# Two homes for two of three tiles of a block's rounded input, and conversions whose scaling names no activation table

## The chip, the cores and the metric

The kernel runs on one core of a Trainium2 chip. The metric is the device time of one execution in microseconds (us), as the median of several runs; lower is better. PE is TensorE, ACT is ScalarE, DVE is VectorE, POOL is GpSimd, SP is SyncE, which issues all DMA transfers.

## The reference, cut to what matters

A decaying linear attention (4 batches, 8 heads, 768 tokens, head size 48) feeds two feed-forward layers of 384 to 2048 to 384 for each of 3072 tokens. All values are float32, and the weights arrive as float64.

```python
for t in range(S):
    state = alpha[:, :, t, :, None] * state + np.einsum('bhd,bhe->bhde', k[:, :, t], v[:, :, t])
    y[:, :, t] = np.einsum('bhd,bhde->bhe', q[:, :, t], state)
x = y.transpose(0, 2, 1, 3).reshape(B * S, H * D)
# layer 1
h = x @ w_in1
g = (a0 + a1*h + a2*h**2 + a3*h**3) / (1 + |b0|*|h| + |b1|*h**2 + 1e-6)
x = g @ w_out1
# layer 2
h = x @ w_in2
g = h * tanh(log1p(exp(h)))
out = g @ w_out2
```

## The kernel before

**Tiling.** The tokens are cut into 6 blocks of 4 x 128. A phase (l, c) is layer l of block c; the 12 phases run in the order of `PHASES`. A phase has 16 steps, one for each 128 columns of the hidden size. A step is a hidden product (`hidden_mms`, L652: three groups k = 0, 1, 2 of three matmuls of 512 columns into one of three PSUM banks), the nonlinear function on ACT, DVE and POOL (`hidden`, L667 to L689), the split of its result g (`split_g`), and an output product (`out_mms`, L701, nine matmuls, into banks 5 to 7). Every float32 factor is split into a rounded part and the rest ("high" and "low"), and three products stand for one.

**The rounded input.** `split_x` makes of a block's input three tiles `xh0`, `xh1`, `xh2` by a rounding copy (L220 on ACT, L222 on DVE) and three tiles `xl0` to `xl2` by a subtraction on DVE (L646). Each of the six tiles has one home, so a phase's copy `xh0` waits until the last hidden product of the phase before has read `xh0`; the same goes for the others.

**Weights.** `load_w` turns a pair of weight tiles from float64 to the split form, 32 times. Sixteen of them (layer 1) fall into the opening and phase (0, 0), sixteen (layer 2) into phases (0, 1) and (1, 0). Each begins on ACT with L327, a scaling written as the function Abs with the table "ln"; after it come either two ACT instructions (L340, L341) and one of DVE (L343), or three of DVE (L329, L331, L333), as `E_CV` says. Later phases stream the converted tiles from DRAM (L371, L372).

**Tables.** ACT's function in layer 2 is Mish (L689), in layer 1 Ln and Exp. `hidden` and L327 name their table, and each change of the named table puts an `ACT_TABLE_LOAD` into ACT's queue (L689 and L799).

**Attention.** Twelve units `attn_unit` (block c, two batches each) work through six levels (L461 on PE, L476 and L496 on DVE, L491 and L485 on ACT), an outer product (L540), outputs (L575 or L611). The first block's two units run before the first hidden product; the others lie among the phases. Filler matmuls (L745) occupy PE until the first hidden product.

**Ends of phases.** `evacuate` copies the three output banks into the ring of three buffers `u` and writes them to DRAM (L714, L712, L715). The first steps of the next layer-1 phase write the same ring (L667).

**What sets the order.** `Plan` gets each instruction with a due time and lists them engine by engine in a small schedule of its own; the due times come from the numbers at the top (`T_PH`, `AT_P`, `D_X`, `LAG`, `W_LEAD` and so on), the engine of a choice from the strings (`E_CV`, `E_HC`, `E_GL0`, `E_GL1`). Each engine then runs its list strictly in order, and SP issues transfers strictly in order.

## Time and profile before

| | |
|---|---|
| median of 3 runs | 1007.2 us (1005.48 to 1007.83) |
| profiled execution, its own time | 1007.53 us |
| its span, first to last instruction | 1005.7 us |
| mean granted TensorE clock | 0.995 |
| PE busy | 965.0 us (96%) |
| DVE busy | 657.2 us (65%) |
| ACT busy | 622.4 us (62%) |
| POOL busy | 309.5 us (31%) |

The time of an execution is its span and some 1.8 us around it. PE's busy time counts pipelined matmuls, so 96% is not 96% of what PE could do: back to back, nine matmuls of 512 columns start 2.04 us after the nine before them. What a change can win here is time in which PE waits.

### The profile page before, as it was taken

To read this page: it belongs to the slowest core of one execution; us is meant where nothing else is said; L and a number is where in the kernel's file an instruction comes from. 1 tells how busy PE (TensorE), PEld (TensorE's weight loads), DVE (VectorE), ACT (ScalarE), POOL (GpSimd) and SP (SyncE) were. 2 spreads that over 40 slices of the span, in tenths; PEclk is the share of its full clock that TensorE was granted. 3 is DMA by queue.
4 is the path that set the end of the run, shared out by engine and by line. 5 is a ranking of instruction groups with operands and counts; after the bars stand their busy time and mean duration, and the time that the engine had idled before them with its cause. 6 is when DMAs were issued, how large, how long until landed. Compare 5 with 4: busy or idle time off the path is not lost.

```text
span 1005.7 us, 24495 instructions
## 1 busy us (share of the span) xinstructions
PE 965.0 (96%) x10370; PEld 779.1 (77%) x10370; DVE 657.2 (65%) x850; ACT 622.4 (62%) x1048; POOL 309.5 (31%) x234
## 2 busy tenths in 40 slices
PE   7998999899999999999999999999999999999998
PEld 6776877677787878888878787767788878888886
DVE  6778999799998899724589733799951189400000
ACT  2787978798878798521498623386621299633332
POOL 2034666442500234334334300143322300043332
PEclk9999999999999999999999999999999999999999
DMA  8385747665768868558638655847446555465530
GB/s 323 120 288 211 261 134 273 220 189 207 254 237 308 299 214 280 166 191 257 211 107 277 192 185 155 292 118 256 118 135 207 149 155 147 136 220 147 176 110 31
DMA packets 75756, 199.98 MB, mean 199 GB/s; under 512 B 8192, under 2 KB 34944, under 8 KB 74112
## 3 DMA queue, kind: packets, MB, share of 16 engines
q1 hardware_dynamic: 75648, 198.43, 60.6%
q8 instruction: 81, 1.33, 0.5%
q14 instruction: 27, 0.22, 0.1%
HBM read 166.94 MB, written 31.46 MB: 197 GB/s over the span
## 4 chain that ended last, share of the span: by engine, by line
PE 64%; DVE 19%; ACT 9%; issue 5%; POOL 2%; DMA 1%; SPq 0%; ACTq 0%; DVEq 0%; POOLq 0%
PE bank L701 29%; PE bank L652 27%; PE pair L461 3%; DVE zp L685 3%; DVE gg L213 2%; DVE zp L676 2%; DVE zp L678 2%; PE bank L745 2%; DVE qka L476 1%; POOL zp L674 1%; PE pair L611 1%; ACT zp L680 1%; ACT zp L673 1%; ACT u L667 1%; ACT zp L684 1%
## 5 line engine op out<-in xcount | busy, mean ns | idle before, releaser
L701 PE MATMUL bank<-gg,wo 128*128 128x512 f32 x1728 | 430.5, 395 | 4.8 <-DVE gg L213 4.0
L701 PEld LDWEIGHTS bank<-gg,wo 128*128 128x128 f32 x1728 | 321.2, 188 | 75.6 <-DVE gg L213 7.7
L652 PE MATMUL bank<-xh,wih 128*128 128x512 f32 x576 | 230.2, 400 | 8.6 <-DVE zp L678 4.3
L652 PE MATMUL bank<-xl,wih 128*128 128x512 f32 x576 | 225.7, 392 | 3.0 <-DVE xl L646 3.0
L652 PE MATMUL bank<-xh,wl 128*128 128x512 f32 x576 | 225.5, 391 | 0.0
L215 POOL TENSOR_TENSOR gg<-zp,gg 128x512 fp32r<-128x512 f32 x80 | 111.8, 1398 | 268.8 <-ACT gg L220 162.7
L674 POOL TENSOR_TENSOR zp<-zp,u 128x512 f32<-128x512 f32 x80 | 125.4, 1568 | 193.1 <-ACT zp L673 192.9
L689 ACT ACTIVATE zp<-bank 128x512 f32<-128x512 f32 x96 | 57.1, 597 | 201.1 <-PE bank L652 201.0
L652 PEld LDWEIGHTS bank<-xh,wih 128*128 128x128 f32 x576 | 108.5, 188 | 34.3 <-DVE zp L678 6.5
L652 PEld LDWEIGHTS bank<-xl,wih 128*128 128x128 f32 x576 | 108.5, 188 | 25.6 <-DVE xl L646 4.4
L652 PEld LDWEIGHTS bank<-xh,wl 128*128 128x128 f32 x576 | 108.5, 188 | 23.3 <-DVE wl L213 0.4
L220 ACT CAST gg<-zp 128x512 fp32r<-128x512 f32 x144 | 89.3, 621 | 43.9 <-PE bank L701 31.0
L213 DVE TENSOR_TENSOR gg<-zp,gg 128x512 fp32r<-128x512 f32 x112 | 86.4, 776 | 34.3 <-ACT gg L220 33.8
L549 POOL TENSOR_TENSOR tmp<-X,qk 48x768 f32<-48x768 f32 x19 | 34.2, 1798 | 177.5 <-DVE X L554 98.2
L676 DVE SCALAR_TENSOR_TENSOR zp<-zp,sc,bank 128x512 f32<-128x512 f32 x96 | 70.9, 740 | 15.1 <-ACT zp L675 14.9
L685 DVE SCALAR_TENSOR_TENSOR zp<-zp,sc 128x512 f32<-128x512 f32 x80 | 72.9, 912 | 10.4 <-ACT zp L684 9.2
L461 PEld LDWEIGHTS pair<-qka 48*64 48x64 f32 (+4 forms) x3840 | 53.7, 125 | 32.1 <-issue 12.0
L680 ACT ACTIVATE zp<-zp,c 128x512 f32<-128x512 f32 x96 | 69.4, 725 | 12.0 <-POOL zp L674 11.9
L667 ACT ACTIVATE u<-bank 128x512 f32<-128x512 f32 x96 | 56.9, 594 | 29.8 <-PE bank L652 25.6
L222 DVE CAST gg<-zp 128x512 fp32r<-128x512 f32 x48 | 25.3, 527 | 75.4 <-ACT zp L689 67.8
L675 ACT ACTIVATE zp<-bank,sc 128x512 f32<-128x512 f32 x96 | 66.1, 688 | 13.1 <-PE bank L652 9.4
L678 DVE SCALAR_TENSOR_TENSOR zp<-zp,sc,bank 128x512 f32<-128x512 f32 x96 | 71.2, 743 | 2.4 <-ACT u L667 0.7
(124 smaller groups left out, 1018.1 us busy)
## 6 DMA issues: line engine op xcount, KB each, us to landing
wo<-woD SPq DMA_DIRECT2D x160, 384.0 KB, 3.3
wl<-wlD SPq DMA_DIRECT2D x160, 192.0 KB, 2.5
qka<-in_qka_dram SPq DMA_DIRECT2D x10, 1536.0 KB, 8.8
woD<-wo SPq DMA_DIRECT2D x16, 768.0 KB, 5.1
raw<-in_w1o_dram SPq DMA_DIRECT2D x8, 768.0 KB, 5.0
raw<-in_w1i_dram SPq DMA_DIRECT2D x8, 768.0 KB, 5.2
wlD<-wl SPq DMA_DIRECT2D x16, 384.0 KB, 5.2
raw<-in_w2i_dram SPq DMA_DIRECT2D x8, 768.0 KB, 4.9
```

Source lines behind the costliest of these rows:

```text
L213: dve(n, due, reads, writes, lambda: nc.vector.tensor_tensor(**kw()))
L215: pool(n, due, reads, writes, lambda: nc.gpsimd.tensor_tensor(**kw()))
L220: act(n, due, reads, writes, lambda: nc.scalar.copy(out=out(), in_=in_()), src="s")
L461: nc.tensor.matmul(bk[j][o:o + m, 32 * g:32 * g + 32].rearrange("p (n l) -> p n l", l=L), lhsT=K[h, e * HC:e * HC + m], rhs=Qv[h, e, :, 1, :],
L652: nc.tensor.matmul(bank[hb], lhsT=w[:, k * P:(k + 1) * P], rhs=x[k], start=(k == 0 and j == 0), stop=(k == KT - 1 and j == 2))
L667: act(NTOK, due, [kh, "tab"], [ku], lambda: nc.scalar.activation(u, h, AF.Abs), table="ln")
L674: pool(NTOK, due, [ku], [kz], lambda: nc.gpsimd.tensor_tensor(out=zs[r], in0=zs[r], in1=u, op=ALU.mult))
L676: dve(NTOK, due, [kh], [kp], lambda: nc.vector.scalar_tensor_tensor(out=ps[r], in0=ps[r], scalar=A2, in1=h, op0=ALU.add, op1=ALU.mult), po ...
L678: dve(NTOK, due, [kh], [kp], lambda: nc.vector.scalar_tensor_tensor(out=ps[r], in0=ps[r], scalar=A1, in1=h, op0=ALU.add, op1=ALU.mult), po ...
L680: act(NTOK, due, [], [kz], lambda: nc.scalar.activation(zs[r], zs[r], AF.Ln, bias=c_1), src="s", ptr=1, table="ln")
L685: dve(NTOK, due, [kw], [kp], lambda: nc.vector.scalar_tensor_tensor(out=ps[r], in0=ps[r], scalar=A0, in1=w(), op0=ALU.add, op1=ALU.mult), ...
L701: nc.tensor.matmul(bank[5 + k], lhsT=wos[b][:, w, k * P:(k + 1) * P], rhs=x[q], start=(f == 0 and j == 0), stop=(f == FT - 1 and j == 2))
```

## The change

1. `xh0`, `xh1`, `xl0`, `xl1` (`KD` = 2 of three tiles) get second homes `xhb0`, `xhb1`, `xlb0`, `xlb1`; phases with an odd number use these. `xh2` and `xl2` keep one home. The room comes from `minus` (now in a buffer of `gg`), from one `ds`, and from `q1`, which now lies in the first buffer `raw0` of the weights.
2. L327 becomes a Copy with the same scale, which names no table. (The sign that Abs dropped is shifted out by the next step.) In ACT's queue 10 table loads stand in place of 22.
3. All numbers of the plan are new. `E_GL1` moves the subtraction of `split_g` in layer 2 of blocks 3, 4 and 5 from POOL to DVE, `E_GL0` that in layer 1 of block 3 from DVE to POOL; the level of 16 of the last block's two attention units is copied on ACT (L491) and not masked on DVE (L496).

```diff
-NLVM = 5
+NLVM = 4
-D_X = 98.985
-D_EV = -36.095
+D_X = 101.394
+D_EV = -62.504
-E_GL0 = 'PVVVVV'
-E_GL1 = 'VPVPPP'
+E_GL0 = 'PVVPVV'
+E_GL1 = 'VPVVVV'
-N16 = 20
+N16 = 24
-R0 = (39.706, 10.751)
+R0 = (48.811, 35.128)
-F_OPEN = 3.25
+F_OPEN = -8.687
...
+KD = 2
...
-    minus = cpool.tile([P, P], F32R, name="minus")
...
+    xb = [[cpool.tile([P, NTOK], F32R, name=f"{n}b{k}") for k in range(KD)] for n in ("xh", "xl")]
+    xsets = [(xh, xl, [""] * KT), (xb[0] + xh[KD:], xb[1] + xl[KD:], ["b"] * KD + [""] * (KT - KD))]
...
+    minus = ghs[NG - 1][:, 0:P]
...
-    q1 = own("q1", [P, 2, 2 * DM])
+    q1 = raws[0].bitcast(F32)
...
-        act(n, due, [kr], [ks], lambda: nc.scalar.activation(st, mag, AF.Abs, scale=F64_SHIFT), src="s", table="ln")
+        act(n, due, [kr], [ks], lambda: nc.scalar.activation(st, mag, AF.Copy, scale=F64_SHIFT), src="s")
...
-    def split_x(l, due):
+    def split_x(l, due, xs):
         src, keys = (xf, XF) if l == 0 else (xg, ["xg"])
+        xh, xl, b = xs
         for k in range(KT):
-            copy(E_X0 if due == V[0] - D_X else E_XH[0], NTOK, due, keys, [f"xh{k}"], lambda k=k: xh[k], lambda k=k: src[:, k, :])
+            copy(E_X0 if due == V[0] - D_X else E_XH[0], NTOK, due, keys, [f"xh{b[k]}{k}"], lambda k=k: xh[k], lambda k=k: src[:, k, :])
...
-            split_x(l, V[i] - D_X)
+            n = PHASES.index((l, c))
+            xs = xsets[n % 2]
+            if n == PHASES.index((1, 0)) + 1:
+                plan.readers["q1"] = plan.readers.get("raw0", []) + [plan.writer["raw0"]]
+            split_x(l, V[i] - D_X, xs)
```

ACT, from the last steps of phase (0, 1) to the start of phase (1, 0), before. `zp` and `u` are buffers of the nonlinear function, `gg` holds g, `xg` is the input of layer 2:

```order
L220 CAST gg_135<-zp_134 128x512
L680 ACTIVATE zp_134<-zp_134,c_1_68 128x512
L220 CAST xh0_107<-xg_106 128x512
L220 CAST xh1_108<-xg_106 128x512
L220 CAST xh2_109<-xg_106 128x512
L684 ACTIVATE zp_134<-zp_134 128x512
```

The three rounding copies stand in a row. In the changed kernel the first two stand 74 instructions ahead of the third, in the middle of phase (0, 1):

```order
L221 CAST gg_138<-zp_137 128x512
L681 ACTIVATE zp_137<-bank2_130,sc_67 128x512
L221 CAST xh0_106<-xg_105 128x512
L221 CAST xh1_107<-xg_105 128x512
L686 ACTIVATE zp_137<-zp_137,c_1_68 128x512
```

and only the third stays where the phase ends:

```order
L673 ACTIVATE u_136<-bank2_130 128x512
L221 CAST gg_138<-zp_137 128x512
L221 CAST wo0_90<-f321_101 128x2x384
L679 ACTIVATE zp_137<-u_136,sc_67 128x512
L221 CAST xh2_108<-xg_105 128x512
L681 ACTIVATE zp_137<-bank2_130,sc_67 128x512
```

Moved: two of the three copies, and with them on DVE the subtractions `xl0` and `xl1`, by a good part of a phase. Phase (1, 2) starts in the same way.

PE, the end of phase (0, 0)'s output products and the first steps of phase (0, 1), before. Banks 5, 6, 7 are the output banks that `evacuate` copies; banks 2, 3, 4 take hidden products:

```order
L652 MATMUL bank2_127<-xh2_109,wih0_1_72 128x512
L652 MATMUL bank2_127<-xl2_112,wih0_1_72 128x512
L652 MATMUL bank2_127<-xh2_109,wl1_88 128x512
L701 MATMUL bank7_132<-gg_135,wo3_94 128x512 x3
L701 MATMUL bank5_130<-gg_135,wo3_94 128x512 x3
L701 MATMUL bank6_131<-gg_135,wo3_94 128x512 x3
L701 MATMUL bank7_132<-gg_135,wo3_94 128x512 x3
L461 MATMUL pair_126<-qka0_145 64x32 x32
L652 MATMUL bank3_128<-xh0_107,wih0_1_72 128x512
```

The last output products of phase (0, 0) come after the third hidden product of phase (0, 1), right ahead of the fourth. In the changed kernel those into banks 5 and 6 come ahead of the first:

```order
L707 MATMUL bank5_133<-gg_138,wo3_93 128x512 x3
L707 MATMUL bank6_134<-gg_138,wo3_93 128x512 x3
L707 MATMUL bank7_135<-gg_138,wo3_93 128x512 x3
L707 MATMUL bank5_133<-gg_138,wo3_93 128x512 x3
L707 MATMUL bank6_134<-gg_138,wo3_93 128x512 x3
L658 MATMUL bank3_131<-xhb0_112,wih0_0_70 128x512
L658 MATMUL bank3_131<-xlb0_114,wih0_0_70 128x512
```

Only the last three, into bank 7, follow after the fourth hidden product. So two of three evacuations can start three hidden products (27 matmuls) earlier, seen from the fourth.

PE, its first rows, before (`cst` is the constant tile of the filler matmuls, `qka` holds q, k and alpha of the first unit, `zp` those of the second):

```order
L745 MATMUL bank_129<-cst 128x256 x4
L429 MATMUL pair<-qka_145 64x64 x32
L745 MATMUL bank_129<-cst 128x256 x5
L461 MATMUL pair<-qka_145 64x32 x32
L745 MATMUL bank_129<-cst 128x256 x3
```

and in the changed kernel:

```order
L751 MATMUL bank_132<-cst 128x256 x8
L432 MATMUL pair<-qka_148 64x64 x32
L751 MATMUL bank_132<-cst 128x256 x5
L464 MATMUL pair<-qka_148 64x32 x32
L432 MATMUL bank_130<-zp 64x64 x2
```

Four more filler matmuls (eight in the profile, which counts each float32 matmul of this kind twice) stand ahead of the first product of the attention. Over the whole opening there are 65 in place of 57. On SP the first two weight loads stand behind all six loads of the two attention units' first tiles and no longer among them, and the load of `q1`, which stood there because nothing held it back, has left the opening.

## Rows read from the trace of the kernel before

**Rows 1.** Stretches of the span: length, busy PE, PEld, DVE, ACT, POOL, clock, DMA, GB/s.

```profile
175.00:200.00 25.00, 20.22 (x317) 15.34 (x316) 19.89 (x24) 18.84 (x37) 12.61 (x12) 0.93 0.66 230
...
245.00:339.00 94.00, 90.08 (x926) 72.19 (x926) 84.65 (x108) 76.38 (x115) 16.79 (x9) 1.00 0.70 250
...
488.00:558.00 70.00, 68.45 (x775) 54.88 (x774) 59.88 (x74) 58.78 (x102) 26.26 (x19) 1.00 0.61 193
...
645.00:724.00 79.00, 73.95 (x822) 58.44 (x822) 76.23 (x102) 56.10 (x93) 25.40 (x17) 1.00 0.59 183
...
863.00:1005.70 142.70, 139.08 (x614) 114.90 (x612) 8.99 (x14) 48.83 (x81) 41.23 (x32) 1.00 0.46 136
```

**Rows 2.** PE in order of time, start of phase (1, 0): start, us, what, [idle before].

```profile
242.66 2.20 PE L701 MATMUL bank<-gg,wo 128*128 128x512 f32 x9
244.70 0.47 PE L652 MATMUL bank<-xh,wih 128*128 128x512 f32 x1
246.56 0.50 PE L652 MATMUL bank<-xl,wih 128*128 128x512 f32 x1 [1.39 <-DVE xl L646]
```

**Rows 3.** ACT in order of time, the same place.

```profile
244.01 1.65 ACT L220 CAST xh<-xg 128x512 fp32r<-128x512 f32 x3
```

**Rows 4.** DVE in order of time, the same place.

```profile
245.82 1.89 DVE L646 TENSOR_TENSOR xl<-xg,xh 128x512 fp32r<-128x512 f32 x3
```

**Rows 5.** PE in order of time, start of phase (1, 2).

```profile
559.80 0.50 PE L652 MATMUL bank<-xl,wih 128*128 128x512 f32 x1 [1.40 <-DVE xl L646]
```

**Rows 6.** PE in order of time, fourth hidden product of phase (0, 1).

```profile
184.65 0.80 PE L652 MATMUL bank<-xh,wih 128*128 128x512 f32 x1 [2.88 <-ACT u L667]
...
187.51 1.13 PE L461 MATMUL pair<-qka 48*60 48x32 f32 x64
```

**Rows 7.** ACT in order of time, the same place.

```profile
179.38 0.59 ACT L714 COPY u<-bank 128x512 f32<-128x512 f32 x1 [0.20 <-PE bank L701]
...
184.00 0.60 ACT L667 ACTIVATE u<-bank 128x512 f32<-128x512 f32 x1 [0.53 <-DMA x2d<-u]
```

**Rows 8.** ACT's groups from 245 to 339 us: xcount, busy us, mean ns, idle before.

```profile
L689 ACT ACT_TABLE_LOAD x7 | 9.0, 1283 | 0.4 <-DVE gg L213 0.3
L799 ACT ACT_TABLE_LOAD x6 | 7.7, 1283 | 0.1
```

**Rows 9.** ACT in order of time inside phase (1, 0).

```profile
271.48 1.28 ACT L799 ACT_TABLE_LOAD   x1
272.77 0.91 ACT L327 ACTIVATE f<-raw 128x768 f32<-128x768 f32 x1
```

**Rows 10.** SP's issues in order of time, at 180 us.

```profile
179.99 0.32 SPq L715 DMA_DIRECT2D x2d<-u  x1
```

**Rows 11.** The chain that ended last, in the opening: start, us, what.

```profile
3.83 3.42 PE bank L745 x8
...
8.34 2.36 PE bank L745 x10
...
77.09 1.12 PE bank L652 x4
```

**Rows 12.** ACT in order of time, in the opening.

```profile
21.21 0.83 ACT L220 CAST wo<-f 128x768 fp32r<-128x768 f32 x1 [10.27 <-DVE f L333]
```

**Rows 13.** DVE in order of time, in the opening.

```profile
33.71 0.99 DVE L421 TENSOR_TENSOR q<-q 128x768 f32<-128x768 f32 x1
```

**Rows 14.** Groups of the whole span: xcount, busy us, mean ns, idle before.

```profile
L685 DVE SCALAR_TENSOR_TENSOR zp<-zp,sc 128x512 f32<-128x512 f32 x80 | 72.9, 912 | 10.4 <-ACT zp L684 9.2
...
L685 DVE SCALAR_TENSOR_TENSOR zp<-zp,sc,bank 128x512 f32<-128x512 f32 x16 | 11.8, 739 | 0.3 <-ACT bank L684 0.2
...
L215 POOL TENSOR_TENSOR gg<-zp,gg 128x512 fp32r<-128x512 f32 x80 | 111.8, 1398 | 268.8 <-ACT gg L220 162.7 <-DVE gg L222 100.8 <-PE bank L701 2.8
...
L213 DVE TENSOR_TENSOR gg<-zp,gg 128x512 fp32r<-128x512 f32 x112 | 86.4, 776 | 34.3 <-ACT gg L220 33.8
```

**Rows 15.** The attention's masked copies from 645 to 800 us: ns min/median/max.

```profile
L496 DVE COPY_PREDICATED AT<-cst,pair x8: 693/718/1323, 648.4 to 738.2; 128x512 f32<-128x512 int32 x8
```

More of the change, by code (lines that the diff above doesn't have):

```diff
@@ L125, in order @@
         heapq.heapify(events)
-        out, busy, loaded = [], {}, 0
+        out, busy, loaded = [], {}, "ln"
         fill, filler = self.fill, None
@@ L272, in attention_moe_kernel, with own @@
     tmp = at_p.tile([P, E2, D], F32, name="tmp")
+    def own(name, shape):
+        return at_p.tile(shape, F32, name=name)
     class Bufs:
@@ L655, in hidden_mms @@
         for k in range(KT):
[L656 removed]
+            pe(0.680, due, [f"wih{l}_{f // 2}", f"wl{a}", f"xh{b[k]}{k}", f"xl{b[k]}{k}"], [f"bank{hb}"], lambda k=k: mms(k))
     def hidden(l, hb, r, i, due):
```

49 lines of the change are left out of this document (24 added, 25 removed).

## The prediction

> **What bounds the kernel now.** I read the stretches of the span first, then PE in order of time wherever PE stands still, then the queue that PE waits for. In the stretches [rows 1] the reader is to see two things. PE is busy nearly throughout, so an instruction saved on ACT, DVE or POOL wins time only where PE waits for that engine; and DVE, not ACT, is the engine that is nearly full where PE loses most after the opening: 84.65 us of 94 from 245 to 339 us, 76.23 of 79 from 645 to 724. From 863 us on DVE has 8.99 us of work in 142.7, and nothing that DVE or POOL does there matters. PE's idle time is small and scattered: 3.92 us from 245 to 339 (94 - 90.08), 1.55 from 488 to 558, 5.05 from 645 to 724, and 4.78 in the 25 us from 175 to 200, where the granted clock is 0.93 as well. The largest single pieces after the opening are these three. At the start of phase (1, 0) PE waits 1.39 us for `xl0` [rows 2], because the three rounding copies start on ACT only at 244.01 [rows 3] and the subtractions only at 245.82 [rows 4], both after the phase before has read the tiles for the last time. The start of phase (1, 2) repeats it with 1.40 us [rows 5]. And at the fourth hidden product of phase (0, 1) PE waits 2.88 us for ACT's L667 [rows 6], which itself waits for a buffer of `u` to be written to DRAM [rows 7]. I sum against the profiled execution's 1007.5 us, 0.3 us above the median.
>
> **The change part by part.**
>
> *Second homes.* No work is added: the same copies and subtractions go to other tiles. What remains at a phase's start is `xh2` and `xl2`: one copy of 0.55 us (1.65 for three [rows 3]) and one subtraction of 0.63 us (1.89 for three [rows 4]), 1.2 us in all. In the changed order PE has nine output matmuls (2.04 us by [rows 2], 242.66 to 244.70) and the six matmuls of k = 0 and 1 (two thirds of that, 1.36 us) between the last reading of the old `xl2` and the first of the new one, so 3.4 us cover 1.2 us, and DVE may be 2.2 us late before PE notices. If that cover is gone, since DVE works off other instructions ahead of `xl2`, the wait returns in part, to at most its old size. The two waits are 1.39 + 1.40 = **2.8 us**; bounds 0 and 2.8. I take the upper bound, since 2.2 us of cover is more than three such subtractions long.
>
> *Tables.* From 245 to 339 us ACT loads tables 13 times at 1.283 us [rows 8], 16.7 us. Of the program's 22 loads 10 remain, and the 12 that vanish all lie here: 12 x 1.283 = 15.4 us of ACT. But ACT is busy for 76.38 of 94 us, and PE's whole idle time here is 3.92 us, of which 1.39 is counted above. So the gain lies between 0 and 2.5 us. DVE is fuller than ACT and keeps its work; what goes is ACT's lateness in feeding it. I take **1.0 us**, nearer to nothing. The row behind a load shows L327 starting at 272.77, 0.01 us after the load of 271.48 ends [rows 9], so a switch costs ACT 1.28 us here and no more. The Trainium skill (ScalarE: Activation LUTs, section What ACT_TABLE_LOAD costs) puts a drain of about 1.38 us on top of each load, 2.66 us for a switch. By that page 12 switches would give ACT 31.9 us back and not 15.4; the trace disagrees, and the bound by PE's idle time would stay.
>
> *Evacuation at 180 us.* Today the output product into bank 5 ends shortly before 179.38, where ACT copies it [rows 7]. The DMA is issued at 179.99 [rows 10], L667 starts at 184.00 and takes 0.60, and PE goes on at 184.65: 5.3 us from that copy to PE. In the changed order PE has, between this output product and the fourth hidden product, one group of bank 6 (0.7 us), three hidden products (6.1 us) and one attention level: nearly 8 us for the same 5.3 us. The wait of 2.88 us goes. During it PE falls idle, and behind it the granted clock is down: six matmuls take from 184.65 to 187.51, 2.86 us [rows 6], in place of 1.36 at the full rate; a mean of 0.93 over 25 us [rows 1] is some 3.5 us at 1.2 GHz. That is another 1.5 us. What is late next is the third evacuation, now behind the fourth hidden product: its buffer returns 5.3 us later, and PE has 5.0 us of work until it needs the bank. A wait of 0.4 us may stay. I take 2.9 + 1.5 - 0.4 = **4.0 us**; bounds 0 (another buffer is late in the same place) and 4.4.
>
> *Opening.* Four more fillers stand ahead of the first attention product, eight matmuls in the profile. Eight at the start take 3.42 us, ten a little later 2.36 [rows 11], so they cost between 1.9 and 3.4 us if the data is there; I take 1.9, as the clock has risen by then. The later weight loads fall into a time in which ACT stood idle for 10.27 us [rows 12], so they cost nothing unless they are later than that. DVE loses the 0.99 us of L421 [rows 13]. Net **+0.9 us**; bounds -3 (ACT no longer blocked behind a conversion) and +4.
>
> *Engines exchanged.* In phase (0, 3) sixteen subtractions of 0.776 us leave DVE for POOL [rows 14], 12.4 us out of a DVE that is busy 59.88 of 70; at most the 1.55 us that PE is idle there. I take **0.8**. In phase (0, 4) two masked copies of 0.72 us [rows 15] leave DVE for ACT, 1.4 us where DVE binds; I take **0.8**, half of what it could be, as DVE waits too. The 48 subtractions that go from POOL to DVE lie mostly where DVE is empty: nothing. At the very end three output products follow the last hidden one, and cover either engine's subtraction.
>
> Sum: -2.8 - 1.0 - 4.0 + 0.9 - 0.8 - 0.8 = -8.5, so 1007.5 - 8.5 = **999.0 us**. With every term at its worse end it is 1007.5 + 4 = 1011.5; at the better ends 2.8 + 2.5 + 4.4 + 1.55 + 1.4 + 3 = 15.7 less, 991.8.
>
> **The rivals.**
>
> *The waits only move.* DVE is full exactly where PE waits. If each wait removed returns at the next step because DVE hasn't become faster, only the clock's 1.5 us and a part of the first term remain, some 2 us: 1005.5, which can't be told from no change, as a measurement of this kernel tells about 0.2% (2 us). For it: the DVE shares [rows 1]. Against: both waits at the starts of phases end on a subtraction that could have been made earlier, and not on a lack of DVE time.
>
> *Slower: the opening.* Everything follows the first hidden product at 77.09 us [rows 11], and the terms behind it sum to -9.4. If the fillers cost 3.4 us at the head of the chain, and the conversions, whose loads now stand behind six loads of attention data, use up the idle 10.27 us [rows 12] and 8.6 us more, the first hidden product comes 12 us later and the time is 1007.5 - 9.4 + 12 = 1010. It decides from a first hidden product at 86.5 us on. For it: PE's queue shows eight more fillers in the opening and no shorter chain. Against: the idle stretch is long, and ACT has fewer conversions that block it.
>
> *Port.* With POOL active, DVE's L685 on two SBUF inputs takes 912 ns, against 739 where one comes from PSUM [rows 14]. If the sixteen subtractions moved to POOL in phase (0, 3), 1.398 us each, shut DVE out while they run, DVE loses 22.4 us and gains 12.4: 69.9 of 70 us, and PE would wait some 3 to 6 us more there; 999.0 + 0.8 + 4.5 = 1004. The Trainium skill (SBUF — State Buffer, section Who interferes with whom) makes this an exclusive lock of the pair that DVE and GpSimd share; 912 against 739 is a slowing, not a full block, so the trace bears out a part.
>
> *More.* If in the freed stretches the scattered waits go as well, above all the 5.05 us from 645 to 724, and the opening shortens by 3 us, the time is 992.
>
> **How the numbers follow.** The forecast, 995 to 1003, has 0.45; *more* 0.15; *port* 0.12; *the waits only move* 0.14; *slower* 0.14. Faster by over 0.2% is the forecast, *more* and most of *port*: 0.71; the same 0.16; slower 0.13. The range reaches from 991, the better ends, to 1008.5, the opening's case at its deciding point, leaving out about 0.15. The likeliest case's own range is 995 to 1003.
>
> **What would show it.** Right: no wait for L646 at the starts of phases (1, 0) and (1, 2); ten table loads in all, one inside phase (1, 0); no idle microsecond of PE at the fourth hidden product of phase (0, 1) and a clock of 1.00 from 175 to 200; a first hidden product between 74 and 81 us. Wrong: a first hidden product beyond 84 us; waits of PE for `gg` or `zp` in phases (1, 0) or (0, 4) that are as long in sum as before; a wait for `u` at the sixth hidden product of phase (0, 1) of more than 1 us.

## The result, and the profile of the changed kernel

The changed kernel takes **1017.89 us** (median of 4 runs, 1015.15 to 1020.39), the kernel before 1006.34 (4 runs): a ratio of **1.0116, with a 95% interval of 1.0088 to 1.0144**. It is slower, where 999.0 was forecast. The profiled execution took 1017.28 us, its span is 1015.5.

To find where the time lies I cut each span at three points that every kernel has: PE's product that makes the second attention unit's state (L540, in the changed kernel L543), the first hidden product (L652, now L658), and the start of phase (0, 1). The stretches of the kernel before (length, busy PE, PEld, DVE, ACT, POOL, granted clock, DMA, GB/s):

```profile
0.00:59.40 59.40, 50.70 (x1191) 40.29 (x1191) 40.22 (x50) 34.46 (x60) 9.28 (x17) 0.97 0.67 243
59.40:77.00 17.60, 14.77 (x448) 12.34 (x448) 15.00 (x20) 13.70 (x18) 8.85 (x8) 1.00 0.75 261
77.00:169.60 92.60, 87.45 (x1331) 69.21 (x1330) 85.36 (x98) 78.41 (x136) 56.79 (x40) 0.98 0.59 214
```

and of the changed kernel:

```profile
0.00:60.00 60.00, 51.80 (x1190) 41.25 (x1191) 36.94 (x44) 31.89 (x54) 10.22 (x17) 0.97 0.55 207
0.00:62.00 62.00, 53.50 (x1197) 42.42 (x1198) 38.45 (x46) 33.89 (x58) 10.22 (x17) 0.97 0.55 210
62.00:86.60 24.60, 21.48 (x453) 17.64 (x453) 18.78 (x22) 13.02 (x18) 5.92 (x8) 0.72 0.72 255
70.30:84.00 13.70, 13.59 (x202) 11.06 (x196) 9.05 (x11) 7.56 (x11) 2.38 (x5) 0.50 0.89 339
86.60:185.10 98.50, 89.44 (x1340) 71.06 (x1339) 88.15 (x103) 84.17 (x145) 58.09 (x41) 0.97 0.58 200
...
175.00:200.00 25.00, 22.97 (x375) 18.53 (x378) 24.18 (x31) 22.38 (x51) 16.14 (x14) 1.00 0.88 307
```

The opening and phase (0, 0) lose 2.6 + 7.0 + 5.9 = 15.5 us; everything behind gives 5.7 back (836.1 us before, 830.4 now). Nine output matmuls moved from phase (0, 1) into (0, 0), 2.0 us by [rows 2], so the honest split is 13.5 lost and 3.7 won. The middle stretch has nearly the same work (448 and 453 matmuls) and takes 7 us more, at a granted clock of 0.72 in place of 1.00.

Where the changes were meant to act, most of what was said came true. PE at the starts of phases (1, 0) and (1, 2), in order of time, shows no wait where [rows 2, 5] show 1.39 and 1.40 us, but at (1, 0) another comes behind it, at 272.21:

```profile
258.81 0.39 PE L658 MATMUL bank<-xh,wih 128*128 128x512 f32 x1
259.03 0.39 PE L658 MATMUL bank<-xl,wih 128*128 128x512 f32 x1
...
272.21 0.80 PE L658 MATMUL bank<-xh,wih 128*128 128x512 f32 x1 [2.76 <-DVE zp L684]
...
570.19 0.39 PE L658 MATMUL bank<-xh,wih 128*128 128x512 f32 x1
570.42 0.39 PE L658 MATMUL bank<-xl,wih 128*128 128x512 f32 x1
```

ACT's groups of table loads: 5 + 4 + 1 = 10, against 22 before (13 of them in [rows 8]):

```profile
L695 ACT ACT_TABLE_LOAD x5 | 6.4, 1283 | 0.1
...
L810 ACT ACT_TABLE_LOAD x4 | 5.1, 1283 | 0.1
...
L736 ACT ACT_TABLE_LOAD x1 | 1.3, 1283 | 0.7 <-PEq L886 0.7
```

In phase (0, 1) the wait for `u` of [rows 6] (2.88 us) is gone. The clock from 175 to 200 us is 1.00 (0.93 in [rows 1]), but the phase starts 15.5 us later here, and the 3.4 us at half clock that began at 184.2 in the kernel before now begin at 203.4. Three other waits are there, the first of them still in phase (0, 0), together 3.78 us:

```profile
181.77 3.47 PE L707 MATMUL bank<-gg,wo 128*128 128x512 f32 x14 [1.19 <-POOL gg L216]
...
199.44 1.08 PE L464 MATMUL pair<-qka 48*60 48x32 f32 x64 [0.73 <-DVE qka L479]
...
202.80 2.83 PE L707 MATMUL bank<-gg,wo 128*128 128x512 f32 x7 [1.86 <-DVE gg L214]
```

### The profile page after: what moved, and what is told of

Same layout as the page of the kernel before. It is cut to its first block, busy times and chain, and to the rows that moved or that the text cites. A ratio compares the mean times of both kernels' runs of the same rounds, so it can differ in the third digit from the quotient of the medians.

```text
span 1015.5 us, 24509 instructions
## 1 busy us (share of the span) xinstructions
PE 975.5 (96%) x10380; PEld 788.0 (78%) x10380; DVE 690.4 (68%) x877; ACT 615.0 (61%) x1046; POOL 262.6 (26%) x202
## 4 chain that ended last, share of the span: by engine, by line
PE 68%; DVE 20%; ACT 7%; issue 4%; DMA 1%; POOL 0%; SPq 0%; ACTq 0%; DVEq 0%; POOLq 0%
PE bank L707 29%; PE bank L658 28%; DVE zp L691 4%; PE pair L464 4%; PE bank L751 3%; DVE zp L682 3%; DVE zp L684 2%; DVE gg L214 2%; DVE qka L479 2%; PE pair L614 1%; DVE AT L499 1%; ACT u L673 1%; ACT gg L221 1%; ACT zp L681 1%; ACT zp L679 1%
## 5 line engine op out<-in xcount | busy, mean ns | idle before, releaser
L214 DVE TENSOR_TENSOR gg<-zp,gg 128x512 fp32r<-128x512 f32 x144 | 106.2, 739 | 126.6 <-ACT gg L221 125.8
L658 PE MATMUL bank<-xh,wih 128*128 128x512 f32 x384 | 154.4, 402 | 7.6 <-DVE zp L691 4.2
L658 PE MATMUL bank<-xl,wih 128*128 128x512 f32 x384 | 150.8, 393 | 0.0
L658 PE MATMUL bank<-xh,wl 128*128 128x512 f32 x384 | 150.7, 392 | 0.0
L216 POOL TENSOR_TENSOR gg<-zp,gg 128x512 fp32r<-128x512 f32 x48 | 72.6, 1514 | 82.5 <-DVE gg L223 47.6
L658 PEld LDWEIGHTS bank<-xh,wih 128*128 128x128 f32 x384 | 72.8, 190 | 24.3 <-DVE zp L684 4.4
L682 DVE SCALAR_TENSOR_TENSOR zp<-zp,sc,bank 128x512 f32<-128x512 f32 x96 | 70.7, 741 | 30.2 <-ACT zp L681 29.9
L658 PEld LDWEIGHTS bank<-xh,wl 128*128 128x128 f32 x384 | 72.7, 189 | 15.5
L658 PEld LDWEIGHTS bank<-xl,wih 128*128 128x128 f32 x384 | 73.0, 190 | 14.7 <-DVE xl L650 0.4
L691 DVE SCALAR_TENSOR_TENSOR zp<-zp,sc 128x512 f32<-128x512 f32 x80 | 81.2, 1018 | 4.1 <-ACT zp L690 2.4
L658 PE MATMUL bank<-xhb,wih 128*128 128x512 f32 x192 | 76.7, 400 | 2.8 <-DVE zp L684 2.7
L464 PEld LDWEIGHTS pair<-qka 48*64 48x64 f32 (+4 forms) x3840 | 54.5, 127 | 27.6 <-issue 12.2
L552 POOL TENSOR_TENSOR tmp<-X,qk 48x768 f32<-48x768 f32 x19 | 31.5, 1658 | 171.5 <-DVE X L557 109.2
L658 PE MATMUL bank<-xlb,wih 128*128 128x512 f32 x192 | 75.1, 391 | 0.0
L658 PE MATMUL bank<-xhb,wl 128*128 128x512 f32 x192 | 74.9, 390 | 0.0
```

Of the source, the lines that this page charges most:

```text
L214: dve(n, due, reads, writes, lambda: nc.vector.tensor_tensor(**kw()))
L216: pool(n, due, reads, writes, lambda: nc.gpsimd.tensor_tensor(**kw()))
L464: nc.tensor.matmul(bk[j][o:o + m, 32 * g:32 * g + 32].rearrange("p (n l) -> p n l", l=L), lhsT=K[h, e * HC:e * HC + m], rhs=Qv[h, e, :, 1, :],
L658: nc.tensor.matmul(bank[hb], lhsT=w[:, k * P:(k + 1) * P], rhs=x[k], start=(k == 0 and j == 0), stop=(k == KT - 1 and j == 2))
L682: dve(NTOK, due, [kh], [kp], lambda: nc.vector.scalar_tensor_tensor(out=ps[r], in0=ps[r], scalar=A2, in1=h, op0=ALU.add, op1=ALU.mult), po ...
L691: dve(NTOK, due, [kw], [kp], lambda: nc.vector.scalar_tensor_tensor(out=ps[r], in0=ps[r], scalar=A0, in1=w(), op0=ALU.add, op1=ALU.mult), ...
```

## Theories and experiments

The chain that ended last, in order of time, shows how the changed kernel comes to its first hidden product:

```profile
63.00 0.87 DVE wo L214
63.87 0.88 DVE f L336
64.78 0.57 DVE wih L223
65.41 2.00 issue
67.41 0.68 DVE qka L438
68.12 1.31 DVE AT L444
69.48 1.26 PE pair L464 x64
71.89 2.73 PE bank L578 x63
75.83 2.00 PE bank L751 x4
77.84 1.86 PE pair L464 x64
80.85 1.28 PE bank L528 x6
82.13 2.70 PE bank L751 x8
84.84 1.01 PE pair L464 x64
86.91 3.19 PE bank L658 x14
```

Behind 62 us DVE works off weight conversions (`wo`, `f`, `wih`) before it makes `qka` and `AT`, from which PE makes the next attention unit's scores; and filler and attention products (L578, L751, L464, L528) stand in PE's queue ahead of L658. The kernel before has the same kinds of products there (its L575, L745, L461 and L525; 448 matmuls, 453 now), so this list names what fills the stretch, and not yet what makes it longer. In the trace the 7 us are PE's: it is busy for 21.48 us in place of 14.77, and for 13.7 us of the stretch it stands at a granted 0.50, which is some 6.8 us. One difference in DVE's queue comes from a part of the change that was not listed: the strings `E_CV`, `E_HC` and `E_LW` are new too, and a conversion with three operations on DVE (L332, L334 and L336, from 61.45 to 64.74) now stands there ahead of `qka` and `AT`; in the kernel before the opening's only one of that kind begins at 10.97 us.

Against this theory, **the order of the queues** at the end of the opening, stood three rivals: **the gap** (PE idles at 65 to 75 us, and the clock falls behind it); **late weights** (the first conversion starts late, since its load stands behind attention data); and, after the first runs, **the redrawn order** (a plan that is made anew is worse by itself, whatever it was changed for). The columns below are the state product of the second unit, the first hidden product, the difference, the start of phase (0, 1), and the rest up to the end of the span, all in us from the profiled execution; the ratio is to the kernel before, measured beside it.

| kernel | state | hidden | diff. | (0, 1) | rest | ratio, 95% interval |
|---|---|---|---|---|---|---|
| before | 59.38 | 77.02 | 17.6 | 169.6 | 836.1 | |
| changed | 61.95 | 86.56 | 24.6 | 185.1 | 830.4 | 1.0116 (1.0088 to 1.0144) |
| a3_opening_of_before | 64.41 | 80.16 | 15.7 | 169.5 | 843.1 | 1.0105 (1.0066 to 1.0144) |
| c3_numbers_of_before | 64.84 | 80.64 | 15.8 | 168.2 | 849.4 | 1.0145 (1.0114 to 1.0175) |
| x1_fillers_in_the_gap | 60.72 | 85.18 | 24.5 | 183.8 | 829.0 | 1.0129 (1.0074 to 1.0183) |
| x6_first_scores_earlier | 62.76 | 85.99 | 23.2 | 184.6 | 831.6 | 1.0107 (1.0070 to 1.0143) |
| r1_first_weights_early | 66.34 | 90.93 | 24.6 | 189.5 | 830.1 | 1.0162 (1.0123 to 1.0201) |
| x2_chain_first | 66.24 | 89.69 | 23.5 | 189.7 | 831.8 | 1.0153 (1.0121 to 1.0184) |
| x2b_first_hidden_first | 63.02 | 78.52 | 15.5 | 182.1 | 831.2 | 1.0087 (1.0054 to 1.0119) |
| x2c_chain_first_waits_kept | 62.90 | 80.77 | 17.9 | 182.4 | 829.0 | 1.0093 (1.0059 to 1.0128) |
| n1_before_nudged_table | 61.19 | 78.17 | 17.0 | 170.7 | 840.1 | 1.0085 (1.0054 to 1.0116) |
| n2_before_nudged_act | 60.64 | 78.32 | 17.7 | 177.6 | 841.7 | 1.0159 (1.0120 to 1.0197) |
| n4_before_nudged_dma | 59.14 | 76.51 | 17.4 | 168.9 | 839.9 | 1.0073 (1.0046 to 1.0101) |
| m2_after_nudged_act | 62.93 | 87.96 | 25.0 | 191.1 | 830.8 | 1.0185 (1.0146 to 1.0224) |
| m4_after_nudged_dma | 60.76 | 84.27 | 23.5 | 186.4 | 830.9 | 1.0124 (1.0046 to 1.0201) |
| h1_one_home_at_two_starts | 64.37 | 88.95 | 24.6 | 187.6 | 831.4 | 1.0126 (1.0106 to 1.0147) |
| c1_copy_without_tables | 60.63 | 78.34 | 17.7 | 169.8 | 835.5 | 0.9992 (0.9971 to 1.0014) |
| bg_chain_first_on_before | 61.97 | 77.73 | 15.8 | 172.9 | 832.4 | 0.9978 (0.9963 to 0.9994) |
| bh_chain_first_on_before | 61.37 | 76.21 | 14.8 | 172.2 | 833.3 | 0.9999 (0.9984 to 1.0014) |
| g2_exchange_and_corners | 62.11 | 79.48 | 17.4 | 170.8 | 831.8 | **0.9959 (0.9936 to 0.9982)** |

Only from c1 on does a row belong to a kernel with before's order held.

**The numbers of before in the changed code.** In a3 the numbers that shape the opening are put back, in c3 all but three.

```diff
# a3, beside T0, AT_P0, F_END, F_RATE, D_CST, E_CV, E_HC, E_LW
-R0 = (48.811, 35.128)
-F_OPEN = -8.687
+R0 = (39.706, 10.751)
+F_OPEN = 3.25
# c3: every number of before, with
+NLVM, N16, KD = 4, 24, 2
```

> The changed kernel with the opening's numbers of before: T0, AT_P0, R0, F_OPEN, F_END, F_RATE, D_CST and the three strings that set the engines of the sixteen weight conversions of each block; homes, copies and all other numbers stay those of the change. The planner makes the order anew from them. Theory 1 (the loss is the replanned order of the opening, 9.5 us until the first hidden product): the first hidden product comes at 75 to 79 us and the time is 1005 to 1010 us. Rival (the loss lies in the new code itself, homes and copies, wherever they stand in the order): the first hidden product stays beyond 83 us, the time 1014 to 1020 us.

> All code of the change with all numbers of before, except that 4 masks and 24 units with copied sixteens stay, as the memory has no room for the fifth mask. Theory 1 (the replanned opening is the loss; homes and copies are worth little in the rest, where the two traces took 925.0 and 924.7 us after the first hidden product): first hidden product at 75 to 79 us, time 1003 to 1008 us. Rival (the new code itself costs): 1012 to 1020 us. My forecast's sum, if its terms for homes and copies were right and only the opening's term was wrong: 997 to 1002 us.

The stretch before the first hidden product fell to 15.7 and 15.8 us, and phase (0, 1) starts at 169.5 and 168.2, as before. By then 117 output matmuls have run where the kernel before has 132, which is 3.4 us by [rows 2]. From the state product to the start of (0, 1) a3 takes 105.1 us, 108.5 with those, the kernel before 110.2 and the changed one, with nine more, 123.1. So the loss behind the state product comes from the opening's numbers and strings, and not from the new code. Theory 1 was wrong all the same on both its forecasts: the first hidden product came at 80.16 and 80.64 where 75 to 79 was said, and the times, 1015.39 and 1018.75, lie where the rival had them, because the rest became 843.1 and 849.4 us, longer than either kernel's. (Behind the first hidden product the two kernels take 928.7 and 928.9 us, not the 925.0 and 924.7 that the expectation names.) Every other number of the plan had found itself another order, so neither run prices one part.

**The gap.** x1 repeats four filler matmuls where PE idled.

```diff
+        fills = [k for k, n in enumerate(out) if ops[n][4] is fill[5]]
+        out[fills[54] + 1:fills[54] + 1] = [out[fills[54]]] * 4
```

> The order of the changed kernel with four more filler products (8 matmuls, 1.9 us at full clock) behind the fifty-fifth, in the 2.1 us in which PE waited before 69.48 us. Theory 2 (the granted clock fell because PE stood idle there; the 13.65 us at half clock from 70.3 on are 4 to 5 of the 9.5 us): no half clock from 70 to 84, first hidden product at 81 to 83 us, time 1012 to 1014.5 us. Rival (the clock falls for what lies earlier, or the tail of the opening waits for ACT and DVE and not for PE): the half clock comes nonetheless or the first hidden product stays at 85.5 to 88 us, time 1016.5 to 1020 us.

Stretches of x1:

```profile
0.00:60.00 60.00, 50.66 (x1195) 40.54 (x1196) 37.85 (x45) 33.09 (x56) 9.31 (x17) 1.00 0.56 206
60.70:85.20 24.50, 20.56 (x461) 17.03 (x461) 18.96 (x22) 13.22 (x18) 5.95 (x8) 0.86 0.76 273
75.10:81.90 6.80, 6.80 (x81) 5.53 (x79) 2.43 (x2) 2.82 (x6) 0.00 (x0) 0.50 1.00 409
```

The half clock came all the same, and in it PE was never idle. It lasted 6.8 us in place of 13.7, and PE waited 2.51 us before the last of its output products (at 74.85) instead. The stretch is 24.5 us as before the edit; the first hidden product is 1.4 us earlier, but the state product, to which the rows are the same, was 1.2 earlier already. The gap falls as the cause of the 7 us, and so does the length of the half clock by itself.

**Earlier scores, earlier weights.** x6 moves two DVE instructions (L438, L444 in the chain above) ahead of one conversion; r1 moves a weight load ahead of the second unit's inputs. `put` moves operations directly ahead of another in the finished order; the kernels below, other than the nudged ones, hold their order in this way.

```diff
+        put(["first2"], "hi6")     # x6
+        put(["load1"], "in1")      # r1
```

> The order of the changed kernel with two DVE operations (the first scale and the masked copy of the first scores of the next unit, 0.68 and 1.30 us) moved ahead of the two conversions that stood before them at 64.78 (0.57 and 2.11 us). Theory 1 with 2 (DVE's order made PE wait until 69.48, and that wait took the clock): PE's next scores start at 67.4, no half clock from 70 on, first hidden product at 79 to 82 us, time 1010 to 1013 us. Rival (the conversions are needed as early as they stood, so the delay comes back at the first hidden products): the first hidden product is earlier by 4 us or more but the time stays at 1015 to 1019 us. Second rival (the order of DVE there is not what bounds): first hidden product at 85 to 88 us.

> The changed kernel's order with one DMA moved: the first load of raw weights is issued ahead of the second unit's inputs, as in the kernel before, instead of behind all inputs of the attention (issued at 7.22 us, landed at 18.5; before 2.58 and 10.0). Theory 1 (the opening is late because ACT idles 14 us for the first weights and the conversions then run behind): the first conversion starts at 9 to 11 us, the first hidden product at 79 to 83 us, time 1010 to 1014.5 us. Rival (the weights have slack up to 45 us; the opening is late for what stands in the queues after 60 us): the conversions start earlier but the first hidden product stays at 85 to 88 us, time 1015 to 1020 us.

x6 won 1.4 us in the stretch (24.6 to 23.2). In r1 the conversion starts at 10.05 us, as wanted, but ACT then waits elsewhere:

```profile
10.05 0.92 ACT L338 ACTIVATE f<-raw 128x768 f32<-128x768 f32 x1 [6.15 <-DMA raw<-in_w1o_dram]
...
20.77 0.92 ACT L338 ACTIVATE f<-raw 128x768 f32<-128x768 f32 x1 [7.82 <-DMA raw<-in_w1i_dram]
...
34.68 1.49 ACT L506 COPY AT<-pair 16x256 f32<-16x256 f32 x4 [11.05 <-PE pair L475]
```

Its state product came at 66.34, but x2, which has no edit up to there, came at 66.24, so r1 does not show that the early load harms. In the stretch behind, which is 24.6 us again, it wins nothing.

**The chain first.** x2 puts the operations that lead from the state product to the first hidden product ahead of conversions and the next unit's levels; x2b moves the first hidden product too; x2c is x2b with two operations back behind what they read. (In x2 and x2b those two read what stood there before, so part of the attention's output is not computed anew.)

```diff
+        put(["decay1", "X1"], "first2")    # x2 and x2b: X1 alone
+        put(["outputs1"], "level2_1")
+        put(["vn1"], "conv8")
+        for x in ("turn1", "xf1", "low8"): # x2, x2b: turn1 there, xf1 ahead of low8
+            put([x], "level2_2")
+        put(["split0"], "merge8")
+        put(["step0"], "level2_4")         # not in x2
```

> The changed kernel's order, in which at the end of the opening the operations of the chain that leads to the first hidden product (second unit: sum for its state on DVE, outputs on PE, their copies on ACT, final transposes on PE, copies to xf on ACT, rounded input on DVE) stand ahead of the next unit's first level and of two weight conversions in their engines' queues; nothing else is moved. Theory 3 (the last 6 of the 9.5 us are what stands before these operations in queues that run in order, with the half clock that the waits bring): outputs at 67.5 to 69 us, first hidden product at 75 to 79 us, time 1006 to 1010 us if the lead is kept to the end. Rival (the loss is the late weight conversions, before 65 us, and what is moved back is needed as soon): first hidden product earlier, but the lead of the phase after it is lost again, time 1013 to 1018 us.

> x2_chain_first with the first hidden product moved ahead of the third attention level of the next unit, behind which it stood (there it came 8 us after its inputs). Theory 3 (order at the end of the opening): the first hidden product comes within 2 us of its first inputs (xh0, xl0), 78 to 82.5 us, and the time is 1009 to 1014. Rival (what the chain gains, the next unit's attention loses in phase (0, 0)): first hidden product at 78 to 82.5, but phase (0, 0) longer by as much, time 1015 to 1021.

> x2b_first_hidden_first with every operation of the chain behind the one that it reads (in x2 and x2b the copies to xf of one unit read before the final transposes, and that unit's state sum before its product, so that their chain was shorter than the real one and a part of the attention's output differed). Theory 3 (the order at the end of the opening is most of the 9.5 us): first hidden product at 79 to 82 us against 86.6, time 1013 to 1016. Rival (with the waits the chain is no faster than in the changed kernel's order): 84 us or more, 1016.5 to 1019.

x2 won 1.1 us in the stretch: the chain on ACT and DVE was shorter, but PE's own queue kept the product behind: PE waits 4.36 us for `AT` in front of the third attention level, and only the last 3.9 us stand at half clock. Its stretch up to 60 us, to which nothing was edited, and that between the two products:

```profile
0.00:60.00 60.00, 51.53 (x1166) 41.02 (x1166) 36.75 (x44) 27.78 (x44) 9.51 (x17) 0.89 0.49 179
...
66.20:89.70 23.50, 17.13 (x453) 14.32 (x453) 19.25 (x24) 12.81 (x18) 7.30 (x8) 0.92 0.73 267
```

With PE's queue changed as well the stretch falls from 24.6 to 17.9 us in x2c, where before has 17.6, at a clock of 1.00 (the first of these stretches of x2c):

```profile
62.90:80.80 17.90, 13.49 (x385) 11.46 (x385) 14.09 (x19) 10.15 (x15) 5.95 (x8) 1.00 0.77 269
80.80:182.40 101.60, 91.19 (x1407) 72.39 (x1406) 92.30 (x106) 87.05 (x147) 57.12 (x41) 0.98 0.61 209
```

So the order of the queues alone can take 6.7 us off the stretch, and PE's is the larger part of it. It is not the order of the kernel before: the third attention level, which stands ahead of the first hidden product in both kernels, stands behind it here, and the stretch has 385 matmuls in place of 453. Phase (0, 0) gives 3.1 back (101.6 after 98.5), as the level that was passed over comes later. The start of (0, 1) moved by 2.7 us of the 15.5, and the ratio of 1.0093 can't be told from the changed kernel's. Of the ten kernels here with the opening's numbers of before none stands at half clock between the two products; of the ten with the changed numbers all do but x2b and x2c. Which row of the order brings the half clock and the 7 us was not isolated.

**The redrawn order.** Each of these changes one cost in the planner by a little and no operation; n stands on the kernel before, m on the changed one.

```diff
-us + 1.4, table
+us + 1.3, table                 # n1
-0.000840
+0.000842                        # n2, m2: us of ACT for an element
-kb / 300.0
+kb / 302.0                      # n4, m4
```

> The kernel of before, with one cost of its planner nudged: a table load at 1.3 us instead of 1.4 (the traces show 1.28). No operation is added or removed; the planner only draws the order anew. Theory 4 (the numbers of before were picked for one order, and any new drawing of the order, by whatever cause, costs some 1 per cent, so that the change's own parts are not the loss): the time 1010 to 1020 us. Rival (a newly drawn order is as good on the mean, so the loss of the change is its own): 1003 to 1009 us.

> The kernel of before, with another cost of its planner nudged: ACT at 0.000842 us for an element instead of 0.000840. No operation is added or removed. Theory 4 (any new drawing of the order costs some 1 per cent): 1010 to 1020 us. Rival (a newly drawn order is as good on the mean): 1003 to 1009 us.

> The kernel of before, with a third cost of its planner nudged: 302 instead of 300 KB for a microsecond of a DMA. No operation is added or removed. Theory 4 (any new drawing of the order costs some 1 per cent, as the two nudges before: 1.0085 and 1.0159): 1010 to 1022 us. Rival (those two were bad luck; the mean of new drawings is that of before): 1001 to 1008 us.

> The changed kernel with the same nudge as n2_before_nudged_act: ACT at 0.000842 us for an element. Theory 4 (the changed kernel is an ordinary drawing, and its parts are worth little or nothing): 1012 to 1024 us, like the nudged ones of before (1014.5 and 1021.4). Rival A (the parts of the change cost by themselves): 1022 to 1032 us. Rival B (the changed kernel was unlucky in its opening alone, and its parts gain some 8 us): 1004 to 1012 us.

> The changed kernel with the same nudge as n4_before_nudged_dma: 302 KB for a microsecond of a DMA. Theory 4: within 6 us of the mean of the nudged kernels of before, 1012 to 1024 us. Rival A (the parts cost by themselves): 1022 to 1032 us. Rival B (the parts gain some 8 us where the opening is not unlucky): 1004 to 1012 us.

Table loads alone follow the order: 26, 24 and 26 in n1, n2 and n4, where the kernel before has 22. Each of the three orders of the kernel before is slower than it, by 0.73 to 1.59%, and the two of the changed one are at 1.24 and 1.85%. The orders of before's numbers start (0, 1) at 168.9 to 177.6 and need 840 to 842 us more; those of the changed numbers start it at 185.1 to 191.1 and need 830 to 831. So two things are shown. Each of three new orders costs before's kernel about as much as the change does. And the changed numbers do have an opening that is slower in all three of their draws and a rest that is shorter in all three.

**One part at a time, order held.** c1 is before with L327 as a Copy that names no table, in the old places. h1 is the changed kernel with one home at the starts of (1, 0) and (1, 2): there `xh0`, `xh1` and their subtractions wait for the phase before again.

```diff
-AF.Abs, scale=F64_SHIFT), src="s", table="ln")
+AF.Copy, scale=F64_SHIFT), src="s", table="ln")          # c1; its table is left out on emission
-            xs = xsets[n % 2]
+            xs = xsets[(n + (n >= 2) + (n >= 6)) % 2][:2] + (xsets[n % 2][2],)   # h1
+            put([f"split{p}"], "next")                    # h1, for p in (2, 6)
```

> The kernel of before with its own order kept on every engine; only the conversions scale by copies that name no table, so that ACT loads 10 tables instead of 22. Forecast (term of 1.0 us): the time 1.0 us shorter, 0.999 of before. Rival A (all 15.4 us of the loads were on the path, as a few steps of phase (1,0) wait for ACT): 5 us or more shorter. Rival B (the waits only move; the loads stood beside PE's work): no change, 0.998 to 1.002. Rival C (the copy is slower on the chip than the former function): conversions of over 0.91 us each and the opening longer.

> The changed kernel's order, with the second homes taken back at the starts of phases (1, 0) and (1, 2) alone: there the rounded input goes into the tiles that the phase before still reads, and its four operations (two on ACT, two on DVE) stand behind that phase's last hidden product, as in the kernel before; no other row moves. Forecast's term (2.8 us for the two waits): PE waits 1.2 to 1.6 us for xl at 258.8 and at 570.2, and phases (0, 1) to (1, 2) together are 2.4 to 3.2 us longer, time 1019.5 to 1021. Rival (the waits only move: without the homes the next waits, for gg and zp, shrink by as much): the waits for xl are there, and the phases together are longer by less than 0.8 us, time 1016.5 to 1019.

c1: 12 table loads less, and no change that can be measured (0.9992). h1, PE in order of time:

```profile
261.06 0.50 PE L668 MATMUL bank<-xhb,wih 128*128 128x512 f32 x1 [0.16 <-ACT xhb L231]
...
262.68 0.50 PE L668 MATMUL bank<-xlb,wih 128*128 128x512 f32 x1 [1.11 <-DVE xlb L660]
...
265.20 0.50 PE L668 MATMUL bank<-xl,wih 128*128 128x512 f32 x1 [0.51 <-DVE xl L660]
...
275.30 0.50 PE L668 MATMUL bank<-xhb,wih 128*128 128x512 f32 x1 [1.19 <-DVE zp L694]
...
574.03 0.50 PE L668 MATMUL bank<-xl,wih 128*128 128x512 f32 x1 [0.20 <-DVE xl L660]
```

The waits for `xhb` and `xl` return at (1, 0), 1.78 us in all, and the wait for `zp` behind them shrinks from 2.76 to 1.19. From (0, 1) to the end of (1, 2) h1 takes 469.8 us (657.4 - 187.6) and the changed kernel 469.9 (655.0 - 185.1). Six more kernels with the same rows there (x1, x6, r1, x2, x2b, x2c) take 468.5 to 470.2, so the 2.4 to 3.2 us of the forecast are not there, and less than some 1.5 us can't be seen in this stretch. At (1, 2) little idle time returns (0.20 us), although the tile has one home there as before; but the nine matmuls of the first hidden product take 2.66 us (571.94 to 574.60) in place of 2.04, and phase (1, 2) takes 85.5 us where the seven others have 84.8 or 84.9. There the second homes are worth some 0.6 us.

**A version from the parts.** g2 is c1 with the subtraction L213 of phase (0, 3) on POOL, and the masked copies of the last two units (L496) as four ACT copies, everything in before's places. bg and bh have c1, the move to POOL and the chain put first as in x2c, but in before's order. (In bg a conversion overwrites a buffer before its last reader, so one pair of block weights differs.)

```diff
# bg, bh, g2: moved is (l, c) == (0, 3), for gl
-nc.vector.tensor_tensor(**kw())
+(nc.gpsimd if moved else nc.vector).tensor_tensor(**kw())
# g2, for the sixteens of the last two units
+for h in range(4):
+    r, o = slice(32 * h, 32 * h + 16), 32 * (h % 2)
+    nc.scalar.copy(out=AT4[r, :, :, o + 16:o + 32], in_=lv[r, :, :, o // 2:o // 2 + 16])
# bg, bh
+put(["X1"], "hi7")
...
+put(["step0"], "level2_4")
```

> c1_copy_without_tables (order of before, copies without tables) with two of the change's exchanges at their old places in the order: gl of phase (0, 3) on POOL instead of DVE, and the masked copies of the sixteens of the last two units (phase (0, 4)) as four copies on ACT instead of one on DVE. Forecast (0.8 us each): phase (0, 3) and the start of (1, 2) together 0.8 us shorter, phase (0, 4) 0.8 shorter, time 0.998 of before. By bg_chain_first_on_before, whose phases from (0, 3) on are of the same order: phase (0, 3) 0.2 and (1, 2) 1.6 us shorter. Rival (the waits only move): phases (0, 3) to (0, 4) together as long as before within 0.5 us, time 0.999 to 1.001.

> c1_copy_without_tables (order of before, copies without tables) with two more edits. At the end of the opening the chain to the first hidden product is moved ahead as in x2b, by a few places on DVE, PE and ACT. And the subtraction that makes gl in phase (0, 3) runs on POOL, at its old place in the order. Forecast of mine for the second (0.8 us): phase (0, 3) from 69.5 to 68.7 us. Rival for it: POOL's operation of 1.40 us in place of DVE's 0.74 comes late for PE, phase (0, 3) 70 to 72. For the first: theory 3 gives the first hidden product at 74 to 75.5 us and, if phase (0, 0) doesn't lose it again, a time of 1002 to 1003.5, 0.997 to 0.998 of before, the first version that beats it; rival (phase (0, 0) loses it): 1004 to 1007.

> bg_chain_first_on_before with the weight buffer kept (there one conversion overwrote it before the last reader). Theory 3: first hidden product at 74.5 to 76.5 us against 77.0 and 78.3; if phase (0, 0) gives 2 to 3 of it back, as in bg (95.2 against 92.6 us) and x2b, the opening and (0, 0) together end within 1 us of before. With the exchange on POOL the time is 0.997 to 0.9985 of before. Rival (phase (0, 0) gives all back and more): 0.9995 to 1.002.

bh has the shortest stretch of all, 14.8 us, and starts (0, 1) at 172.2: what is won before the first hidden product is lost in phase (0, 0) (95.9 us against 92.5), the same that x2c showed. g2 is faster than both kernels, 1003.74 us against 1006.3 for the kernel before beside it. The stretches of phases (0, 3), (1, 2) and (0, 4) in c1:

```profile
488.10:557.70 69.60, 68.09 (x773) 54.46 (x772) 59.98 (x74) 58.87 (x102) 26.29 (x19) 1.00 0.61 192
557.70:644.40 86.70, 85.11 (x909) 68.96 (x907) 39.55 (x53) 32.73 (x57) 11.65 (x9) 1.00 0.62 192
644.40:723.70 79.30, 74.29 (x823) 58.67 (x824) 76.53 (x102) 56.38 (x93) 25.66 (x18) 1.00 0.59 182
```

and in g2:

```profile
488.20:557.50 69.30, 67.78 (x773) 54.53 (x772) 57.34 (x62) 60.09 (x103) 43.66 (x32) 1.00 0.61 193
557.50:642.60 85.10, 84.83 (x910) 69.08 (x909) 38.95 (x49) 32.10 (x56) 14.73 (x12) 1.00 0.63 195
642.60:721.10 78.50, 74.09 (x823) 58.80 (x824) 75.75 (x101) 57.68 (x97) 25.92 (x18) 1.00 0.59 185
```

They sum to 235.6 and 232.9 us: the two exchanges are worth 2.7. bh has the first of them alone, and there the same rows as g2 but for the copies. Its three phases sum to

```profile
sum 233.70, PE 227.00 PEld 182.25 DVE 172.78 ACT 148.54 POOL 83.98; mean PE 75.67 PEld 60.75 DVE 57.59 ACT 49.51 POOL 27.99
```

so the move to POOL is worth 1.9 us and the copies 0.8. Of the 1.9, 1.6 lie in (1, 2): the wait at its start (1.36 us for `xl` in c1) goes without second homes, because DVE no longer has the subtractions of (0, 3) ahead of `xl`.

## Why the prediction was wrong, by its own steps

**The opening, the step that failed.** It stood at "Net **+0.9 us**", with +4 as its worse end. Measured: the first hidden product 9.5 us later (77.02 to 86.56), the start of (0, 1) 13.5 net. The fillers were priced about right: PE's first attention product comes at 9.96 us in place of 7.18, 2.8 us later, where 1.9 to 3.4 was said. The later loads were said to "cost nothing unless they are later than that", that is, later than ACT's idle 10.27 us, and r1, which takes the first one back, wins nothing in the stretch. The step went wrong by what it left out: the rest of the opening's order up to the first hidden product, the strings that move conversions between engines, and the clock. None of them has a term. Three pieces make the 13.5 us. 7.0 us lie between the two products. a3 and c3, with the opening's numbers and strings of before, have that stretch at 15.7 and 15.8 us, so these make it (shown). In the changed kernel it is PE at half clock, and x2c takes 6.7 us off it by moving operations alone; which number, string or row does it is not shown. 2.6 us at the state product lies inside the spread of 60.72 to 66.24 which seven kernels with the same rows up to there show (the changed one, x1, x2, x2b, x2c, x6, h1; seven with before's rows have 59.38 to 62.11), so the change may have made it or not. 3.9 us net is in phase (0, 0). Its cause stays open: 6.8 us of the phase stand at half clock (3.4 before), and the third hidden step waits 4.23 us for L691's `zp` at 100.00, but no run took that apart. 17 conversions were started before (0, 1) in either kernel, 8 of them in phase (0, 0) now and 7 before.

**Slower: the opening, the rival.** Its place and its point were right: the product came at 86.56, on the 86.5 from which it was to decide. (At that point its own sum gives 1007.5, and not the 1008.5 that the range's end names.) Its mechanism was not: the fillers cost 2.8 us, and with the first load early r1 has the same stretch. It had 12 us later there and 9.4 us of gains behind, and gave 1010; measured are 13.5 and 3.7, so the gains fell short as well.

**Second homes, 2.8 forecast, some 0.6 measured.** Both waits went, as said, and 3.4 us of cover did hide the third subtraction. But at (1, 0) the wait came back behind it (2.76 us for `zp`), and without second homes it is shorter by nearly as much (1.57 us for 1.78): DVE binds there. That is the rival *the waits only move*; against it stood that the subtractions "could have been made earlier, and not on a lack of DVE time". g2 shows the opposite for (1, 2): less DVE work, and the wait goes. The changed kernel has that exchange too, so the sum counted this wait under second homes alone, where two parts of the change remove it.

**Tables, 1.0 forecast.** A load takes 1283 ns as read, and c1's interval runs from 2.9 us won to 1.4 lost, so it holds both nothing and the 1.0. Phase (1, 0), where the loads lay, takes 93.0 us in c1 and 92.9 to 93.4 in bg, bh and g2, against 94.3 before. That fits the 1.0, but kernels with the changed order and the same rows differ by 1.6 us there (89.7 to 91.3), so it is not shown.

**Evacuation, 4.0 forecast, 1.4 measured.** Phase (0, 1) went from 75.1 to 73.7 us with the same 831 matmuls: nine output matmuls left it at its start and nine came at its end. The `u` wait went as foretold, but part of its gain went to the waits for `gg` and `qka` shown above, and the half clock, whose 1.5 us the term had counted as won, came all the same behind another wait, at 203.4 in place of 184. The kernels with before's rows there differ by 1.5 us in this phase (74.4 to 75.9), so the 1.4 are uncertain.

**Engines exchanged, 1.6 forecast, 2.7 measured** in g2, with before's order: 1.9 for the move to POOL and 0.8 for the copies, where 0.8 each was said. (Of the two masked copies one stands in phase (1, 3), at 738.22, and not in (0, 4).) The *port* rival's loss did not come: POOL takes 1514 ns for a subtraction (1398 in [rows 14]) and DVE's two-SBUF form 1018 ns (912), as the groups of the changed kernel show:

```profile
L691 DVE SCALAR_TENSOR_TENSOR zp<-zp,sc 128x512 f32<-128x512 f32 x80 | 81.2, 1018 | 4.1 <-ACT zp L690 2.4
...
L216 POOL TENSOR_TENSOR gg<-zp,gg 128x512 fp32r<-128x512 f32 x48 | 72.6, 1514 | 82.5 <-DVE gg L223 47.6 <-ACT gg L221 25.1 <-issue 8.6
```

but PE's time in (0, 3) is no longer for it. The rival's mechanism is there, though. In (0, 3) the two-SBUF form takes 962 ns in c1 and 1179 ns in g2:

```profile
L686 DVE SCALAR_TENSOR_TENSOR zp<-zp,sc 128x512 f32<-128x512 f32 x13 | 12.5, 962 | 2.4 <-ACT zp L685 2.3
...
L691 DVE SCALAR_TENSOR_TENSOR zp<-zp,sc 128x512 f32<-128x512 f32 x13 | 15.3, 1179 | 3.7 <-ACT zp L690 3.6
```

and DVE's busy time there falls by only 2.64 us (59.98 to 57.34) for sixteen subtractions less, 12.4 us by [rows 14]. Most of what DVE was to win is taken back by slower instructions, and PE does not wait for it. Single instructions do show more: DVE's L214 for `wl`, usually 0.95 us, took 2.11 from 65.37 while POOL's L552 ran from 65.05 to 66.67, and ended 0.81 us after it. The Trainium skill (SBUF — State Buffer, section Who interferes with whom) has DVE and GpSimd shut each other out of one pair of ports; this row agrees, the mean over many instructions is only a slowing.

**Open.** Which number, string or row of the opening brings the 7.0 us and their half clock; phase (0, 0)'s 3.9 us; and why a cost nudged by a little loses 0.73 to 1.59%. The last may be selection, since the kernel before was the better order of many, but that is argued, not shown.

## What to carry to other kernels

Before the first product that bounds the rest, read each engine's queue instruction by instruction up to that product, and give a term to all that stands ahead of it on PE and DVE and to every string that moves work between engines, not only to the fillers and the loads. A change that makes a planner draw its order anew carries a price of its own, here about 1%: nudge a cost without changing an operation to learn it, and to learn what a part is worth hold the order and change that part alone. A wait that ends on the fullest engine can come back behind it until that engine has less to do, as at (1, 0) here.
